# Order and halves of token block 2's output sums, and the engine of its y's lower parts, in a retention and feed-forward kernel

## The chip, the cores and the metric

The kernel runs on one core of a Trainium2 chip. The metric is device time in microseconds of one execution, as the median of several runs. In what follows TensorE is PE in the rows (PEld is its weight load), VectorE is DVE, ScalarE is ACT, GpSimd is POOL and SyncE is SP.

## What is computed

A linear attention with decay (2 batches, 8 heads, 768 positions, 64 features a head) gives x, and two feed-forward nets follow. Cut to what matters:

```python
def _moe_ref(x, w_in, w_out):            # x: 1536 x 512, w_in: 512 x 2048
    h = x @ w_in
    g = np.where(h >= 1, h, np.where(h <= -1, 0.0, (h + 1) ** 2 / 4))
    return g @ w_out                     # y: 1536 x 512

def _moe2_ref(y, w_a, w_b, w_out):       # w_a, w_b: 512 x 1536
    return ((y @ w_a) * (y @ w_b)) @ w_out

def reference(**inputs):
    x = attention(q, k, v, lam).transpose(0, 2, 1, 3).reshape(1536, 512)
    return _moe2_ref(_moe_ref(x))        # everything in float32
```

## The kernel before

**Precision.** A float32 number is carried as two tiles for TensorE: a high part (ScalarE casts it, line 265) and a low part, the remainder (line 266, a subtraction with two SBUF inputs, on GpSimd unless another engine is given). `split_act` issues the two one after the other. `mm3` (line 354) forms a product from three matmuls per pair: high by high, high by low, low by high. Every matmul of the feed-forward stages is issued at line 358; it has 128 rows, a 128x128 weight load of its own and 512 moving columns.

**Tokens.** The 1536 tokens are three blocks of 512 (nb = 0, 1, 2). Features are four groups of 128 (m or k = 0 to 3).

**PSUM.** There are eight banks of 512 columns. One (`words`) is a scratch for the weights' preparation. Seven are handed out in rotation by `bank()`; a product may start in its bank when the reader of the bank's content before has finished.

**First net.** `h_bank` makes one tile of g, `y_bank` (line 467) sums four tiles' contribution to one group m of y: 12 matmuls into a bank, then `gather` (line 464, VectorE) adds the bank to y's running sum in SBUF. In the last group of tiles (`last`) `y_bank` also splits the finished y of blocks 0 and 2 and half of block 1 into the tiles `block0` to `block2`, from which the second net's products read. Blocks 0 and 1 also go through `strassen_tokens` (lines 401 to 405), which prepares sums for a Strassen scheme.

**Second net.** From here on three of the seven banks are `held`: they collect the output of token block 2, m = 1, 2, 3, over all six groups, without a sum on VectorE. Four banks rotate. `both_banks` (line 413) makes one tile of g for all three blocks, in nine products: called s, u, a (block 2 with w_a, 12 matmuls), s again, w, f, b (block 2 with w_b, 12 matmuls), d, g in the order of issue; the others have six. VectorE adds at line 426, multiplies at 440, 444 and 451, and the result is split by `give_g`. `o_stage` (line 509) then calls `o_bank` (line 489) for m = 0, 1, 2, 3: six matmuls each. For blocks 0 and 1, and for block 2's m = 0, they go into a rotating bank and are gathered (line 464; in the first group line 462, a copy on ScalarE); for block 2's m = 1, 2, 3 they go into the held bank. The stage of block 2 for one group stands between the next group's two calls of `both_banks`; the last one ends the program. In the last group the sums are sent to the output: gathered ones as 128x512 on SyncE's queue (line 499), held ones as two halves, the first copied by VectorE and sent on SyncE's queue, the second copied by ScalarE and sent on ScalarE's (lines 506 and 507).

**Background.** The weights arrive as 64-bit numbers and are prepared tile by tile in small steps that `bg()` puts between the products: ScalarE at lines 280 and 281, VectorE at 294, 298, 302 and 311 (a custom instruction with two SBUF inputs), then a split; for pairs of tiles VectorE also forms four sums of 128x256 (line 333). Each engine takes its instructions in the order in which the code issues them, so the calls of `bg` set where these steps stand among the sums.

Of the kernel before, what the change touches and what calls it, by code (L numbers as in the profile page):

```python
# [22 lines left out]
DM = H * D  # L23
KT = DM // 128
NB = 3
# [10 lines left out]
def retention_ffn_kernel(ctx: ExitStack, tc: tile.TileContext, lam, att, w1i, w1o, w2ab, w2o, out):  # L36
# [7 lines left out]
    nc = tc.nc  # L44
# [16 lines left out]
    def bank():  # L61
        banks.rotate(-1)
        return banks[-1]
# [3 lines left out]
    def t2(name):  # L67
        return two.popleft()

    def free2(*tiles):  # L70
        two.extend(tiles)
# [60 lines left out]
    xy = {}  # L132
# [131 lines left out]
    def split_act(src, hi, lo, engine=None):  # L264
        nc.scalar.copy(hi, src)  # L265
        (engine or nc.gpsimd).tensor_tensor(out=lo, in0=src, in1=hi.bitcast(F32), op=ALU.subtract)  # L266
# [76 lines left out]
    def bg(n=1):  # L343

        for _ in range(n):
            if at["tile"] < min(at["limit"], len(order)):
                at["tile"] += next(stream)
# [6 lines left out]
    def mm3(ps, pairs, start=True, stop=True):  # L354
        n = len(pairs)
        for i, (l, r) in enumerate(pairs):
            for j, (a, b) in enumerate(((0, 0), (0, 1), (1, 0))):
                nc.tensor.matmul(out=ps, lhsT=l[a], rhs=r[b],   # L358
                                 start=(start and i == 0 and j == 0), stop=(stop and i == n - 1 and j == 2))
# [96 lines left out]
    acc = {}  # L456

    def gather(total, ps, first):

        if first:  # L460
            total = t2("acc")
            nc.scalar.copy(total, ps)
        else:
            nc.vector.tensor_tensor(out=total, in0=total, in1=ps, op=ALU.add)  # L464
        return total

    def y_bank(g, nb, m, last):
        ps = bank()
        fts = range(4 * g, 4 * g + 4)
        mm3(ps, [([wt["1o", f][:, a, m * 128:(m + 1) * 128] for a in range(2)],  # L470
                  [gt[1, f, nb][:, b, :] for b in range(2)]) for f in fts])
        y = acc["y", nb, m] = gather(acc.get(("y", nb, m)), ps, g == 0)
        if last:
            xy[nb] = [block[nb][:, k] for k in range(KT)]
            if nb != 1 or m >= 2:
                split_act(y, xy[nb][m][:, 0], xy[nb][m][:, 1])
            if nb == 2:
                free2(acc.pop(("y", nb, m)))

# [9 lines left out]
    def o_bank(g, nb, m, last):  # L489
        fts = range(2 * g, 2 * g + 2)  # L490
        r0 = nb * TB + m * 128
        pairs = [([gt[2, f, nb][:, a, m * 128:(m + 1) * 128] for a in range(2)],
                  [wt["2o", f][:, b] for b in range(2)]) for f in fts]
        if m not in held or nb < NB - 1:
            ps = bank()
            mm3(ps, pairs)
            o = acc["o", nb, m] = gather(acc.get(("o", nb, m)), ps, g == 0)
            if last:
                nc.sync.dma_start(out=out[r0:r0 + 128], in_=o)
            return  # L500
        mm3(held[m], pairs, g == 0, last)
        if last:
            o = t2("o")
            for i, copy, queue in ((0, nc.vector.tensor_copy, nc.sync), (1, nc.scalar.copy, nc.scalar)):
                cols = slice(i * DM // 2, (i + 1) * DM // 2)
                copy(o[:, cols], held[m][:, cols])
                queue.dma_start(out=out[r0:r0 + 128, cols], in_=o[:, cols])

    def o_stage(g, nb, pieces):
        last = g == FF2 // 256 - 1  # L510
        for m in range(KT):
            o_bank(g, nb, m, last)
            bg(pieces)
        for f in range(2 * g, 2 * g + 2):
            four.append(gt.pop((2, f, nb)))
            if nb == NB - 1:
                four.append(wt.pop(("2o", f)))
# [105 lines left out]
    def y_stage(g, nb, ms=range(KT), between=lambda m: None):  # L623
        for m in ms:
            y_bank(g, nb, m, g == FF1 // 512 - 1)
            between(m)
            bg()
        y_done(g, nb)

    y_stage(0, 0)  # L630
    for i in range(2, len(stages)):
        g, nb = stages[i]
# [16 lines left out]
    for g in range(groups):  # L649
        at["limit"] = 32 + 6 * g + 6  # L650
        done(32 + 6 * g + 2)
        both_banks(2 * g)
        at["limit"] = 32 + 6 * g + 8
        if g:
            o_stage(g - 1, 2, 2)
        done(32 + 6 * g + 4)
        both_banks(2 * g + 1)
        at["limit"] = 32 + 6 * g + 10
        done(32 + 6 * g + 6)
        o_stage(g, 0, 1)  # L660
        o_stage(g, 1, 1)
# [47 lines left out]
```

## Time and profile before

| what | us |
|---|---|
| runs: median (lowest to highest of 3) | 619.71 (618.56 to 620.05) |
| the profiled execution | 620.09 |
| its span in the trace | 618.3 |
| TensorE busy in it | 597.7 |
| VectorE busy in it | 457.3 |
| GpSimd busy in it | 278.5 |
| ScalarE busy in it | 267.8 |

The profiled execution's own time is 1.8 us longer than the span that the trace covers. Times in rows are counted from the span's start. A row of the timeline gives start, length, engine, line, operation, what it writes and reads, the shape, how many were merged, and in brackets how long the engine was idle before and what ended that. Matmuls are pipelined: a merged row's length is its last end less its first start, and starts show the pace.

### The profile page before, as it was taken

How to read it: one execution, taken by the hardware profiler on the slowest of the kernel's cores; microseconds unless marked ns; L12 is line 12 of the kernel's file. 1: busy time of each engine (PE TensorE's matmuls, PEld its weight loads, DVE VectorE, ACT ScalarE, POOL GpSimd, SP SyncE). 2: the span in 40 equal slices, each digit the busy share in tenths (PEclk: the TensorE clock that was granted, in tenths of full speed). 3: DMA queues.
4: the chain of work that ended last, by engine and by line, in shares of the span. 5: the costliest groups of instructions: out<-in, count | busy, mean ns of one | idle time of the engine just before them, and what ended most of it. 6: DMA issues, size and time to landing. Idle time of an engine off the chain costs nothing.

```text
span 618.3 us, 8380 instructions
## 1 busy us (share of the span) xinstructions
PE 597.7 (97%) x3100; PEld 488.4 (79%) x3100; DVE 457.3 (74%) x684; ACT 267.8 (43%) x473; POOL 278.5 (45%) x218
## 2 busy tenths in 40 slices
PE   7797899999999999999999999999999999999997
PEld 3676678888888888888888788888888888888886
DVE  1578861964975786497869997989979979979553
ACT  1245552655642553264545456434424424424110
POOL 3535570443522543352947655553453553543420
PEclk9799899999999999999999999999999999999999
DMA  5965520221310212131101222302302202300004
GB/s 176 378 247 203 184 92 1 75 96 68 103 64 10 98 68 69 34 103 49 55 1 35 68 87 83 103 34 90 95 21 96 92 18 93 100 14 1 0 23 182
DMA packets 20937, 52.72 MB, mean 85 GB/s; under 512 B 2584, under 2 KB 4896, under 8 KB 20896
## 3 DMA queue, kind: packets, MB, share of 16 engines
q1 hardware_dynamic: 19624, 51.52, 24.3%
q10 hardware_dynamic: 1272, 0.67, 0.4%
q8 instruction: 24, 0.39, 0.3%
q14 instruction: 17, 0.14, 0.1%
HBM read 49.03 MB, written 3.15 MB: 84 GB/s over the span
## 4 chain that ended last, share of the span: by engine, by line
PE 82%; DVE 8%; ACT 4%; POOL 2%; issue 2%; DMA 1%; ACTq 0%; DVEq 0%; POOLq 0%
PE ps L358 79%; DVE words L294 1%; PE ps L225 1%; PE ps L221 1%; DVE two L302 1%; DVE words L298 1%; DVE two L401 1%; DMA lamp<-in_lam 1%; ACT words L280 1%; DVE two L311 1%; PE ps L150 1%; DVE two L180 1%; DMA rows<-base 1%; ACT four L265 1%; ACT two L281 0%
## 5 line engine op out<-in xcount | busy, mean ns | idle before, releaser
L266 POOL TENSOR_TENSOR four<-two,four 128x512 fp32r<-128x512 f32 x109 | 143.1, 1319 | 213.6 <-ACT four L265 203.4
L358 PE MATMUL ps<-block,four 128*128 128x512 f32 x828 | 196.9, 391 | 1.4 <-POOL block L266 1.4
L358 PEld LDWEIGHTS ps<-block,four 128*128 128x128 f32 x828 | 154.6, 188 | 35.4 <-POOL block L266 1.8
L358 PE MATMUL ps<-four,four 128*128 128x512 f32 x633 | 162.0, 389 | 0.0
L358 PEld LDWEIGHTS ps<-four,four 128*128 128x128 f32 x633 | 118.7, 188 | 24.9 <-issue 0.2
L265 ACT CAST four<-two 128x512 fp32r<-128x512 f32 x109 | 67.1, 620 | 93.4 <-DVE two L451 23.7
L266 POOL TENSOR_TENSOR late_four<-two,late_four 128x512 fp32r<-128x512 f32 x47 | 62.2, 1329 | 56.8 <-ACT late_four L265 49.5
L358 PE MATMUL ps<-block,late_four 128*128 128x512 f32 x324 | 77.2, 389 | 0.0
L358 PEld LDWEIGHTS ps<-block,late_four 128*128 128x128 f32 x324 | 60.8, 188 | 12.6
L280 ACT ACTIVATE words<-raw 128x512 f32<-128x512 f32 x68 | 43.1, 634 | 55.0 <-DVE two L302 49.7
L358 PE MATMUL ps<-four,late_four 128*128 128x512 f32 x243 | 64.0, 389 | 0.0
L377 ACT ACTIVATE two<-two,half 128x512 f32<-128x512 f32 x42 | 30.2, 720 | 70.4 <-DVE two L376 70.4
L294 DVE TENSOR_SCALAR words<-words 128x512 f32<-128x512 f32 x68 | 47.0, 691 | 17.4 <-ACT words L280 17.4
L358 PE MATMUL ps<-late_four,four 128*128 128x512 f32 x213 | 58.5, 389 | 0.0
L358 PEld LDWEIGHTS ps<-four,late_four 128*128 128x128 f32 x243 | 45.6, 188 | 9.5
L464 DVE TENSOR_TENSOR two<-two,ps 128x512 f32<-128x512 f32 x62 | 42.2, 680 | 13.1 <-PE ps L358 13.1
L311 DVE CUSTOM_DVE_ANT_0 two<-two,two 128x1024 uint16<-128x1024 uint16 x54 | 49.7, 921 | 1.9
L376 DVE TENSOR_SCALAR two<-ps 128x512 f32<-128x512 f32 x42 | 28.7, 684 | 29.9 <-PE ps L358 29.4
L298 DVE TENSOR_SCALAR words<-words 128x512 int32<-128x512 int32 x68 | 47.5, 699 | 2.3
L426 DVE TENSOR_TENSOR two<-two,ps 128x512 f32<-128x512 f32 x50 | 32.9, 682 | 19.2 <-PE ps L358 16.7
L358 PEld LDWEIGHTS ps<-late_four,four 128*128 128x128 f32 x213 | 40.0, 188 | 8.3
L265 ACT CAST late_four<-two 128x512 fp32r<-128x512 f32 x47 | 28.9, 620 | 36.4 <-DVE two L440 11.4
(99 smaller groups left out, 596.3 us busy)
## 6 DMA issues: line engine op xcount, KB each, us to landing
load<-in_att SPq DMA_DIRECT2D x48, 256.0 KB, 5.3
raw<-in_w2ab SPq DMA_DIRECT2D x24, 512.0 KB, 3.2
raw<-in_w1i SPq DMA_DIRECT2D x16, 512.0 KB, 3.4
raw<-in_w1o SPq DMA_DIRECT2D x16, 512.0 KB, 3.3
raw<-in_w2o SPq DMA_DIRECT2D x12, 512.0 KB, 3.2
out<-two SPq DMA_DIRECT2D x7, 256.0 KB, 2.0
dmask<-rows SPq DMA_DIRECT2D x2, 256.0 KB, 4.6
out<-late_two SPq DMA_DIRECT2D x2, 256.0 KB, 2.0
```

Source lines behind the costliest of these rows:

```text
L150: nc.tensor.matmul(out=sc[c][h % 2][:, pr * CH:(pr + 1) * CH], lhsT=kT[p0:p0 + 64, pr * CH:(pr + 1) * CH], rhs=qT[p0:p0 + 64, pr * CH:(pr ...
L265: nc.scalar.copy(hi, src)
L266: (engine or nc.gpsimd).tensor_tensor(out=lo, in0=src, in1=hi.bitcast(F32), op=ALU.subtract)
L280: nc.scalar.activation(out=words, in_=r[:, :, 1].bitcast(F32), func=ACTF.Abs)
L294: nc.vector.tensor_scalar(out=words, in0=words, scalar1=HIGH_MIN, scalar2=HIGH_MAX, op0=ALU.max, op1=ALU.min)
L298: nc.vector.tensor_scalar(out=word, in0=word, scalar1=3, scalar2=0x3FFFFFFF, op0=ALU.logical_shift_left, op1=ALU.bitwise_and)
L311: nc.vector.tensor_tensor(out=v, in0=v, in1=c, op=ALU.add)
L358: nc.tensor.matmul(out=ps, lhsT=l[a], rhs=r[b], start=(start and i == 0 and j == 0), stop=(stop and i == n - 1 and j == 2))
L376: nc.vector.tensor_scalar(out=r, in0=ps, scalar1=-1.0, scalar2=1.0, op0=ALU.max, op1=ALU.min)
L377: nc.scalar.activation(out=r, in_=r, func=ACTF.Square, scale=0.5, bias=half)
L426: add = lambda o, x, ps: nc.vector.tensor_tensor(out=o, in0=x, in1=ps, op=ALU.add)
L464: nc.vector.tensor_tensor(out=total, in0=total, in1=ps, op=ALU.add)
```

## The change

Three things. In the last group `y_bank` gives block 2's low parts to VectorE and no longer to GpSimd. `o_stage` calls `o_bank` for m = 1, 2, 3, 0 and no longer 0, 1, 2, 3, for all blocks and groups; for blocks 0 and 1 all four go into rotating banks as before. And in the last group the sum of block 2's m = 0, now the program's last, is made in two halves of 256 columns, each in a bank of its own, with its own six matmuls, its own gather on VectorE and its own transfer, the first on SyncE's queue and the second on ScalarE's.

```diff
@@ -473,7 +473,7 @@
         if last:
             xy[nb] = [block[nb][:, k] for k in range(KT)]
             if nb != 1 or m >= 2:
-                split_act(y, xy[nb][m][:, 0], xy[nb][m][:, 1])
+                split_act(y, xy[nb][m][:, 0], xy[nb][m][:, 1], nc.vector if nb == 2 else nc.gpsimd)
             if nb == 2:
                 free2(acc.pop(("y", nb, m)))
 
@@ -492,11 +492,18 @@
         pairs = [([gt[2, f, nb][:, a, m * 128:(m + 1) * 128] for a in range(2)],
                   [wt["2o", f][:, b] for b in range(2)]) for f in fts]
         if m not in held or nb < NB - 1:
-            ps = bank()
-            mm3(ps, pairs)
-            o = acc["o", nb, m] = gather(acc.get(("o", nb, m)), ps, g == 0)
-            if last:
-                nc.sync.dma_start(out=out[r0:r0 + 128], in_=o)
+            parts = 2 if last and nb == NB - 1 else 1
+            for i in range(parts):
+                ps = bank()
+                cols = slice(i * DM // parts, (i + 1) * DM // parts)
+                mm3(ps[:, cols], [(l, [x[:, cols] for x in r]) for l, r in pairs])
+                if parts == 1:
+                    o = acc["o", nb, m] = gather(acc.get(("o", nb, m)), ps, g == 0)
+                else:
+                    o = acc["o", nb, m]
+                    gather(o[:, cols], ps[:, cols], False)
+                if last:
+                    (nc.scalar if i else nc.sync).dma_start(out=out[r0:r0 + 128, cols], in_=o[:, cols])
             return
         mm3(held[m], pairs, g == 0, last)
         if last:
@@ -508,7 +515,7 @@
 
     def o_stage(g, nb, pieces):
         last = g == FF2 // 256 - 1
-        for m in range(KT):
+        for m in (1, 2, 3, 0):
             o_bank(g, nb, m, last)
             bg(pieces)
         for f in range(2 * g, 2 * g + 2):
```

On VectorE, in the stage of y's last sums for block 2 (`block_73` is `block2`, `two_...` are y's running sums and weight tiles, `ps_112` to `ps_115` the four rotating banks):

```order
 L464 TENSOR_TENSOR two_93<-two_93,ps_112 128x512
+L266 TENSOR_TENSOR block_73<-two_93,block_73 128x512
 L294 TENSOR_SCALAR words<-words 128x512
 L298 TENSOR_SCALAR words<-words 128x512
 L464 TENSOR_TENSOR two_105<-two_105,ps_113 128x512
+L266 TENSOR_TENSOR block_73<-two_105,block_73 128x512
 L302 SCALAR_TENSOR_TENSOR two_109<-raw,words 128x512
 L464 TENSOR_TENSOR two_110<-two_110,ps_114 128x512
+L266 TENSOR_TENSOR block_73<-two_110,block_73 128x512
 L311 ISA two_109<-two_109,two_94 128x1024
 L464 TENSOR_TENSOR late_two_942<-late_two_942,ps_115 128x512
+L266 TENSOR_TENSOR block_73<-late_two_942,block_73 128x512
```

Each low part stands directly behind the sum of the same m, ahead of the next step on the weights and of the next sum.

On GpSimd, at the same place (`late_four_936` is the low part's tile of the weights that line 311 makes):

```order
 L405 TENSOR_TENSOR block_72<-two_108,block_72 128x512
-L266 TENSOR_TENSOR block_73<-two_93,block_73 128x512
-L266 TENSOR_TENSOR block_73<-two_105,block_73 128x512
-L266 TENSOR_TENSOR block_73<-two_110,block_73 128x512
 L266 TENSOR_TENSOR late_four_936<-two_109,late_four_936 128x512
-L266 TENSOR_TENSOR block_73<-late_two_942,block_73 128x512
 L266 TENSOR_TENSOR four_74<-two_99,four_74 128x512
```

The four low parts are gone, and the weight tile's low part follows the work on the Strassen sums.

On TensorE, at the program's end (`ps_116`, `ps_117` and `ps_111` are the held banks, `ps_113` and `ps_114` rotating ones):

```order
-L358 MATMUL ps_113<-late_four_937,four_76 128x512 x3
-L358 MATMUL ps_113<-four_86,four_77 128x512 x3
 L358 MATMUL ps_116<-late_four_937,four_76 128x512 x3
 L358 MATMUL ps_116<-four_86,four_77 128x512 x3
@@ -780,3 +778,7 @@
 L358 MATMUL ps_111<-late_four_937,four_76 128x512 x3
 L358 MATMUL ps_111<-four_86,four_77 128x512 x3
-L705 UNCONDITIONAL_BRANCH
+L358 MATMUL ps_113<-late_four_937,four_76 128x256 x3
+L358 MATMUL ps_113<-four_86,four_77 128x256 x3
+L358 MATMUL ps_114<-late_four_937,four_76 128x256 x3
+L358 MATMUL ps_114<-four_86,four_77 128x256 x3
```

The six matmuls of m = 0 leave the first place, and twelve of half the width end the program.

## Rows read from the trace of the kernel before

**Rows 1.** The page, part 1: busy us (share of the span) xinstructions.

```profile
PE 597.7 (97%) x3100; PEld 488.4 (79%) x3100; DVE 457.3 (74%) x684; ACT 267.8 (43%) x473; POOL 278.5 (45%) x218
```

**Rows 2.** Chain that ended last, in order of time: start, us, what; a long piece.

```profile
407.57 207.10 PE ps L358 x912
```

**Rows 3.** TensorE's waits (us, times, longest), then its timeline at the first both_banks.

```profile
PE ps L358 <- POOL block L266: 1.4, 1, 1.4
...
336.30 1.52 PE L358 MATMUL ps<-four,four 128*128 128x512 f32 x6
337.65 2.43 PE L358 MATMUL ps<-block,four 128*128 128x512 f32 x10
341.44 1.89 PE L358 MATMUL ps<-block,four 128*128 128x512 f32 x7 [1.36 <-POOL block L266]
```

**Rows 4.** Timeline of VectorE from the sum of m = 0 on.

```profile
332.55 0.68 DVE L464 TENSOR_TENSOR two<-two,ps 128x512 f32<-128x512 f32 x1
333.15 0.69 DVE L294 TENSOR_SCALAR words<-words 128x512 f32<-128x512 f32 x1
333.87 0.70 DVE L298 TENSOR_SCALAR words<-words 128x512 int32<-128x512 int32 x1
334.48 0.68 DVE L464 TENSOR_TENSOR two<-two,ps 128x512 f32<-128x512 f32 x1
335.08 0.68 DVE L302 SCALAR_TENSOR_TENSOR two<-raw,words 128x512 int32<-128x512 int32 x1
...
336.27 1.47 DVE L311 CUSTOM_DVE_ANT_0 two<-two,two 128x1024 uint16<-128x1024 uint16 x1
337.66 0.67 DVE L464 TENSOR_TENSOR late_two<-late_two,ps 128x512 f32<-128x512 f32 x1
338.26 0.69 DVE L294 TENSOR_SCALAR words<-words 128x512 f32<-128x512 f32 x1
...
340.92 1.02 DVE L311 CUSTOM_DVE_ANT_0 two<-two,two 128x1024 uint16<-128x1024 uint16 x1
```

**Rows 5.** Timeline of ScalarE: casts of m = 0 and 2, and what precedes.

```profile
333.26 0.62 ACT L265 CAST block<-two 128x512 fp32r<-128x512 f32 x1 [2.22 <-DVE two L464]
...
335.79 0.65 ACT L280 ACTIVATE words<-raw 128x512 f32<-128x512 f32 x1
...
336.91 0.62 ACT L265 CAST block<-two 128x512 fp32r<-128x512 f32 x1
```

**Rows 6.** Timelines of VectorE and GpSimd in strassen_tokens, the same subtraction.

```profile
323.06 0.68 DVE L405 TENSOR_TENSOR four<-two,four 128x512 fp32r<-128x512 f32 x1
323.83 1.61 DVE L405 TENSOR_TENSOR late_four<-two,late_four 128x512 fp32r<-128x512 f32 x1
...
323.27 1.62 POOL L405 TENSOR_TENSOR four<-two,four 128x512 fp32r<-128x512 f32 x1 [1.29 <-ACT four L403]
```

**Rows 7.** Timelines of VectorE and TensorE up to the second both_banks.

```profile
345.73 1.27 DVE L426 TENSOR_TENSOR two<-two,ps 128x512 f32<-128x512 f32 x2
...
351.00 0.68 DVE L444 TENSOR_TENSOR late_two<-late_two,ps 128x512 f32<-128x512 f32 x1
...
352.92 1.52 PE L358 MATMUL ps<-four,four 128*128 128x512 f32 x6
```

**Rows 8.** Timeline of the program's end, and a 128x256 sum from PSUM.

```profile
614.70 0.42 DVE L506 COPY two<-ps 128x256 f32<-128x256 f32 x1 [0.87 <-PE ps L358]
615.16 0.37 ACT L506 COPY two<-ps 128x256 f32<-128x256 f32 x1 [0.92 <-DVE two L506]
615.56 0.34 ACTq L507 DMA_DIRECT2D out<-two  x1
...
91.64 0.42 DVE L209 TENSOR_TENSOR st<-st,ps 128x256 f32<-128x256 f32 x1 [0.27 <-ACT st L208]
```

**Rows 9.** Weight loads by form (busy us, mean ns), and a timeline's row.

```profile
L358 PEld LDWEIGHTS ps<-four,late_four 128*128 128x128 f32 x243 | 45.6, 188 | 9.5
...
89.74 0.60 PEld L194 LDWEIGHTS ps<-load,two 128*64 128x64 f32 x16
```

## The prediction

> **What bounds the kernel now.** I read the busy time by engine first: TensorE is busy for 597.7 of the 618.3 us, VectorE for 457.3 [rows 1]. Then the chain that ended last: its last long piece is 207 us of matmuls without a break [rows 2]. Then TensorE's waits: of all matmuls of the feed-forward stages (line 358) one waited, for 1.36 us, and for GpSimd [rows 3]. So a change can win only that one wait, something at the very end, or less work on TensorE, and anything that makes TensorE wait is paid in full, because nothing behind it has slack to give back. The timelines around the wait and at the end show the rest.
>
> The wait: the last four banks of y (token block 2, features m = 0 to 3) are summed by VectorE (line 464), rounded to a high part by ScalarE (line 265, the cast), and the remainder is the low part (line 266, GpSimd). The third product of the first both_banks reads all four. It issues ten of its twelve matmuls at 337.65 and stands until GpSimd has the low part of m = 3; the eleventh starts at 341.44 [rows 3]. Ten matmuls at the pace of the row above it (six in 1.35 us, 0.226 each) would have ended at 339.92: TensorE loses 1.52 us here. VectorE is no less full: from 332.55 on its rows follow one another without a wait [rows 4].
>
> **Part 1: the low parts move to VectorE.** Off GpSimd go four instructions of about 1.3 us; onto VectorE come four of 0.68 us, the length of the same subtraction on VectorE where it was not disturbed [rows 6]. VectorE takes its queue in order, and each low part stands directly behind its own sum and needs the cast, which needs that sum. So VectorE stands still for each cast. Behind it in the queue are the next weight tile's steps and the next sum, and for the sums TensorE waits, since the products reuse those banks.
>
> The path, from the sum of m = 0 at 332.55 to 333.23 [rows 4], with 0.03 to 0.04 us for each hand-over (the sum ends at 333.23, the cast starts at 333.26) [rows 4, 5]:
> - cast 333.26 to 333.88 (0.62, unchanged) [rows 5]; low part of m = 0: 333.91 to 334.59.
> - Starts follow one another on VectorE by 0.60 after a sum, 0.72 and 0.61 across the two word steps (lines 294, 298) [rows 4]: word steps at 334.51 and 335.23, sum of m = 1 at 335.84 to 336.52. Cast to 337.17, low part 337.20 to 337.88.
> - Line 302 at 337.80, sum of m = 2 at 338.40 to 339.08 (0.60 each). ScalarE now does the next tile's lines 280 and 281, which waited for line 302; from the start of 280 to the cast of m = 2 is 336.91 - 335.79 = 1.12 us [rows 5], so from 338.51 the cast starts at 339.63 and ends at 340.25. Low part of m = 2: 340.28 to 340.96.
> - Line 311 at 340.88, this time undisturbed, sum of m = 3 at 341.48 to 342.16. ScalarE first casts the weight tile (341.6 to 342.2), then m = 3: to 342.82.
> - GpSimd starts the low part of that weight tile at about 342.25. Where two such instructions (both inputs in SBUF) meet on VectorE and GpSimd, one stands until the other is done: the subtraction that took 0.68 us took 1.61 beside a GpSimd instruction that had started before it [rows 6]. GpSimd is first here, by over half a microsecond. So the low part of m = 3 runs from about 343.51 to 344.19.
>
> TensorE's eleventh matmul then starts at 344.23 and not at 341.44: **+2.8 us**, in place of a wait that is shortened. That TensorE stands earlier as well (for the banks of m = 1 and m = 2, sums at 336.52 and 339.08, where the products would have come at 336.30 and 337.9) is inside this number. Bounds: without GpSimd in the way the low part starts at 342.85 and the term is +2.1; with a second instruction in the way it is 1.3 more, +4.1. I take 2.8, by the order and the row.
>
> **Part 2: what VectorE's delay does next.** After the low part come the same instructions as before, from line 294 (338.26) to line 311 (340.92), 2.66 us [rows 4]. They now start at 344.11; line 311 starts at 346.77, and ends at 347.46 where it ended at 341.94 (then 1.02 long). VectorE is 5.52 us late, TensorE 2.8. Until line 444 (351.00 to 351.68) no row of VectorE waited for TensorE. The first product that waits for line 444 is the second one of the next both_banks, which takes the bank that line 444 reads; it started at 352.92 [rows 7], with 1.24 us to spare. Now line 444 ends at 351.68 + 5.52 = 357.20, the product starts at 357.24: TensorE is **4.3 us** late in all, 1.5 more than at the first wait. This holds if the stretch between lines 311 and 444 keeps its length, with its two collisions with GpSimd: four short instructions of line 333 lie between 341.94 and the sum at 345.73 [rows 7], 3.8 us. They are put in motion by line 311 on both engines, so I expect them again. If both collisions go, that stretch is about 2.5 us shorter, VectorE's lateness is under 2.8 + 1.24, and the term is zero: bounds 0 and +1.5, taken +1.5. Later VectorE waits for TensorE again; from there on both are late by the same amount, and TensorE, without gaps, gives nothing back.
>
> **Part 3: the order of the sums.** In five of the six o_stages of block 2 the bank of m = 0 goes from first to last; 6 matmuls of 0.226 us change places with 18. On VectorE its sum moves behind six background steps, and on ScalarE, in the first of these stages, its copy. I cost this at nothing: the bank is wanted again by the fourth product of the next both_banks, 6 + 6 + 12 = 24 matmuls or 5.4 us after the last matmul of m = 0, and the six steps that VectorE now does first are ready while TensorE is still at the other three banks. If that cover were gone, each of the five stages would pay one sum of 0.68 us, 3.4 in all.
>
> **Part 4: the end.** Before, the last bank is one that is held: after the last matmul VectorE copies the first half (614.70, 0.42), ScalarE the second only after that (615.16, 0.37), and ScalarE's queue sends it at 615.56 [rows 8]. Now the last piece is half of the bank of m = 0, and its sum is one VectorE instruction of 128x256 with one input in PSUM: 0.42, as in line 209 [rows 8]. It is sent at 614.70 + 0.42 + 0.04 = 615.16: **-0.40 us**. Landing stays: the same two queues, 128 KB each. All copies of held banks, ScalarE's and SyncE's transfers move 1.36 us ahead of the end, and hide under the last matmuls.
>
> The price is TensorE's: twelve matmuls of 256 columns with twelve weight loads, in place of six of 512 with six. At half of 0.226 each they take the same 1.36 us. A weight load's row is 188 ns long, longer than 113; if loads could not overlap one another, twelve would take 2.26 us, +0.9. Against that stands the row of 16 loads of 64 columns in 0.60 us, 38 ns apart [rows 9], 75 for 128 columns. Bounds 0 and +0.9; I take **+0.1**, near that row. The Trainium skill ("TensorE: Matmul & The Clock Gate", the section on LDWEIGHTS and the mechanism in Part 3) has a load at columns / 1.2 ns, 107 for 128 columns, and lets it overlap a matmul only in another row group. By that, an estimate, the six added loads would cost 0.64 us, and the sum would be 0.5 higher. This trace does not agree for 512 columns, where six matmuls with their loads take 1.35 us.
>
> **Sum.** 2.8 + 1.5 + 0 - 0.4 + 0.1 = +4.0 us. The profiled execution took 620.09 us: 624.1. The median of the runs is 619.71, 0.38 lower: **623.7**. About 0.3%, 1.86 us, is what a measurement of this kernel can tell from no change: 617.85 to 621.57.
>
> **Rivals.**
> - A: the lateness of VectorE is caught up before line 444 (its collisions with GpSimd fall elsewhere). Then 2.8 - 0.3 = +2.5: 622.2. For it: GpSimd has four instructions fewer. Against it: the instructions that collide there are the same and start from the same event.
> - B, not slower: VectorE never stands, because ScalarE's casts are ready when it gets to them, and with GpSimd empty line 311 needs 0.69 and not 1.47 [rows 4]. Then the sum of m = 3 starts at 337.66 - 0.78 + 3 x 0.60 = 338.68, its low part ends at about 340.1, and of the 1.52 us only 0.2 is left. With the end: -1.3 - 0.3, 618.1; with the wait wholly gone 617.8. It decides at the instruction between sum and low part: with any two in between there would be time for the cast. The order has none, so I give it little.
> - C: as A, but the weight tile's low part does not get in front of that of m = 3. Then 2.1 - 0.3 = +1.8: 621.5, at the edge of what can be told from no change.
>
> **How the numbers follow.** Forecast 0.58, A 0.20, C 0.14, B 0.08. The likeliest's own range is 622.5 to 625.0 (its terms less 1.2, and 0.9 for the loads with some of the second collision). For 8 in 10 it must reach A and the upper part of C: 620.9 to 625.3. Slower by over 0.3%: forecast and A, 0.78. Within: C and part of B, 0.16. Faster: 0.06.
>
> **What would show it.** In the changed kernel's trace: VectorE idle before each of the four low parts until ScalarE's cast, about 0.7 us for m = 0 and 1, 1.3 and more for m = 2 and 3; TensorE's waits up to the eleventh matmul 4.3 us in all (1.52 before), and 1.5 more by the next both_banks; the last low part of y at 1.3 us or starting late behind GpSimd; the last transfer on ScalarE's queue 0.4 us sooner after the last matmul; twelve matmuls about 0.113 apart. I am wrong if VectorE starts a low part without a gap, or if TensorE's wait at that product is under 1.5 us.

## The result and the profile after

The changed kernel takes 625.70 us (median of 6, 624.83 to 626.60) against 619.88 us of the kernel before (6 runs beside it, 617.88 to 621.14). The ratio is 1.0099, with a 95% interval of 1.0082 to 1.0117: 6.1 us more, 5.1 to 7.3. The direction was forecast, the size was not: the sum said +4.0 us and the upper end of the range was 625.3.

One thing must be known to read the two traces side by side. The attention's first 95 us, which no edit touches, differ by up to 2.4 us between the profiled executions; in that of after, the feed-forward part starts 2.14 us sooner than in that of before, and the matmuls up to y's last sums all keep this difference. So the time of a row of after is compared here with its row of before less 2.14, which is called the row's old place. The profiled execution of after took 624.85 us, with a span of 623.1.

The page's first part, which answers to [rows 1]:

```profile
PE 599.0 (96%) x3106; PEld 487.7 (78%) x3106; DVE 462.5 (74%) x689; ACT 267.6 (43%) x473; POOL 273.6 (44%) x214
```

TensorE's waits in the feed-forward part (us in total, times, longest), which answer to the first line of [rows 3]:

```profile
PE ps L358 <- ACT two L428: 1.2, 2, 0.6
...
PE ps L358 <- ACT block L265: 1.1, 1, 1.1
PE ps L358 <- ACT words L280: 0.9, 1, 0.9
PE ps L358 <- DVE block L266: 0.9, 1, 0.9
PE ps L358 <- ACT late_two L428: 0.6, 1, 0.6
PE ps L358 <- DVE two L464: 0.2, 1, 0.2
```

One wait of 1.4 us for GpSimd has become seven. Four of them (L464, L280, the cast L265, L266) belong to y's last sums. The one put down to L280 ends at 337.12, 0.15 us behind VectorE's sum of m = 2 (not shown), whose bank the product takes; the first ends 0.14 behind the sum of m = 1. The other three name line 428, ScalarE's copy of product s, and come later, at 454.40, 501.53 and 548.66. The prediction has no word of line 428.

VectorE's timeline of after at y's last sums, from the sum of m = 0 on, which answers to [rows 4]; the last row is line 444 of [rows 7]:

```profile
330.42 0.68 DVE L464 TENSOR_TENSOR two<-two,ps 128x512 f32<-128x512 f32 x1
331.78 0.69 DVE L266 TENSOR_TENSOR block<-two,block 128x512 fp32r<-128x512 f32 x1 [0.69 <-ACT block L265]
...
338.16 0.69 DVE L266 TENSOR_TENSOR block<-two,block 128x512 fp32r<-128x512 f32 x1 [1.19 <-ACT block L265]
...
340.73 1.32 DVE L266 TENSOR_TENSOR block<-late_two,block 128x512 fp32r<-128x512 f32 x1 [0.69 <-ACT block L265]
...
354.38 0.68 DVE L444 TENSOR_TENSOR late_two<-late_two,ps 128x512 f32<-128x512 f32 x1
```

GpSimd's timeline there:

```profile
340.24 1.27 POOL L266 TENSOR_TENSOR late_four<-two,late_four 128x512 fp32r<-128x512 f32 x1 [8.59 <-issue]
```

TensorE's timeline there, which answers to [rows 3]; the last row is the product u of [rows 7]:

```profile
342.11 3.08 PE L358 MATMUL ps<-block,four 128*128 128x512 f32 x8 [0.86 <-DVE block L266]
344.99 2.19 PE L358 MATMUL ps<-four,four 128*128 128x512 f32 x6
...
355.21 1.62 PE L358 MATMUL ps<-four,four 128*128 128x512 f32 x6
```

VectorE idles before each low part until ScalarE has cast the sum just made (before that of m = 1, not shown, for 0.69 us). The last low part takes 1.32 and not 0.68, because GpSimd's instruction started 0.49 us before it and ended at 341.51. TensorE's eleventh matmul starts at 342.11; its old place is 341.44 - 2.14 = 339.30, so it is 2.81 us late. Its next matmuls are slow as well: six from 344.99 on span 2.19 us, where [rows 3] has 1.52 for six. The table of stretches shows why (from:to, the length, the busy time of PE, PEld, DVE, ACT and POOL, the granted clock, DMA share, GB/s):

```profile
341.00:342.90 1.90, 1.04 (x4) 0.67 (x4) 1.86 (x3) 0.19 (x1) 0.51 (x1) 1.00 0.00 0
342.90:346.40 3.50, 3.50 (x10) 2.74 (x9) 3.33 (x7) 2.25 (x5) 0.35 (x1) 0.51 0.35 121
346.40:348.00 1.60, 1.60 (x9) 1.29 (x8) 1.60 (x2) 0.58 (x2) 1.60 (x2) 1.00 0.18 69
```

The granted clock is 0.51, its lower level of 1.2 GHz, in the 3.5 us just behind the four waits, and back at 1.00 behind that. After that TensorE is 4.4 to 4.5 us behind its old place, and stays so until the first wait for line 428. Taken over the matmuls between the steps (medians over at least 170 starts), its lateness goes 4.54, 5.41, 6.28, 7.15: three steps of 0.87, 2.6 us in all.

The end, from the timeline of all engines, which answers to [rows 8]:

```profile
618.16 0.52 PE L358 MATMUL ps<-late_four,four 128*128 128x256 f32 x3
...
619.23 0.52 PE L358 MATMUL ps<-four,four 128*128 128x256 f32 x3
...
619.79 0.42 DVE L464 TENSOR_TENSOR two<-two,ps 128x256 f32<-128x256 f32 x1 [0.30 <-PE ps L358]
620.24 0.34 ACTq L506 DMA_DIRECT2D out<-two  x1
```

Nine half matmuls take 619.23 - 618.16 = 1.07 us, 0.119 each; from VectorE's last instruction to the last transfer's issue are 0.45 us, where [rows 8] had 0.86.

### The profile page after: what moved, and what is told of

It reads as the page before. It is cut to its first block, busy times and chain, and to the rows that moved or that the text cites. A ratio compares the mean times of both kernels' runs of the same rounds, so it can differ in the third digit from the quotient of the medians.

```text
span 623.1 us, 8399 instructions
## 1 busy us (share of the span) xinstructions
PE 599.0 (96%) x3106; PEld 487.7 (78%) x3106; DVE 462.5 (74%) x689; ACT 267.6 (43%) x473; POOL 273.6 (44%) x214
## 5 line engine op out<-in xcount | busy, mean ns | idle before, releaser
L266 POOL TENSOR_TENSOR four<-two,four 128x512 fp32r<-128x512 f32 x109 | 143.2, 1320 | 213.8 <-ACT four L265 202.4
L358 PE MATMUL ps<-four,four 128*128 128x512 f32 (+1 forms) x636 | 163.3, 390 | 1.4 <-ACT two L428 1.2
L265 ACT CAST four<-two 128x512 fp32r<-128x512 f32 x109 | 67.0, 619 | 94.4 <-DVE two L451 23.5
L266 POOL TENSOR_TENSOR late_four<-two,late_four 128x512 fp32r<-128x512 f32 x47 | 62.2, 1327 | 68.1 <-ACT late_four L265 50.0
L280 ACT ACTIVATE words<-raw 128x512 f32<-128x512 f32 x68 | 43.1, 634 | 56.4 <-DVE two L302 49.8
L358 PE MATMUL ps<-late_four,four 128*128 128x512 f32 (+1 forms) x216 | 58.7, 386 | 0.0
L464 DVE TENSOR_TENSOR two<-two,ps 128x512 f32<-128x512 f32 (+1 forms) x63 | 42.3, 672 | 17.0 <-PE ps L358 17.0
L265 ACT CAST late_four<-two 128x512 fp32r<-128x512 f32 x47 | 29.0, 621 | 40.1 <-DVE two L440 11.3
L426 DVE TENSOR_TENSOR two<-two,ps 128x512 f32<-128x512 f32 x52 | 34.2, 682 | 15.8 <-PE ps L358 12.1
```

The lines of the kernel that those rows point to most:

```text
L280: nc.scalar.activation(out=words, in_=r[:, :, 1].bitcast(F32), func=ACTF.Abs)
L358: nc.tensor.matmul(out=ps, lhsT=l[a], rhs=r[b], start=(start and i == 0 and j == 0), stop=(stop and i == n - 1 and j == 2))
L426: add = lambda o, x, ps: nc.vector.tensor_tensor(out=o, in0=x, in1=ps, op=ALU.add)
```

## Where the three late waits come from

Line 428 is ScalarE's copy of the bank of s, and product w takes that bank next. In ScalarE's queue the copy stands behind the casts of the weight sums that VectorE makes at line 333. The place is the stage of block 2 for the second group and the second call of both_banks around it; the same happens one and two groups later.

The timeline of all engines in the kernel before, at this place:

```profile
446.46 0.69 DVE L311 CUSTOM_DVE_ANT_0 two<-two,two 128x1024 uint16<-128x1024 uint16 x1
...
447.16 4.24 PE L358 MATMUL ps<-block,late_four 128*128 128x512 f32 x18
447.25 0.42 DVE L333 TENSOR_TENSOR two<-two 128x256 f32<-128x256 f32 x1
...
447.71 2.19 DVE L333 TENSOR_TENSOR two<-two,two 128x256 f32<-128x256 f32 x3
...
448.23 1.39 POOL L266 TENSOR_TENSOR four<-two,four 128x512 fp32r<-128x512 f32 x1 [1.68 <-PE ps L358]
...
449.94 0.62 ACT L265 CAST late_four<-two 128x512 fp32r<-128x512 f32 x1 [1.15 <-DVE two L333]
450.47 0.58 ACT L428 COPY late_two<-ps 128x512 f32<-128x512 f32 x1
...
451.24 1.54 PE L358 MATMUL ps<-four,late_four 128*128 128x512 f32 x6
```

The same in after, with the sum of m = 0 (line 464) now in between:

```profile
448.26 0.69 DVE L311 CUSTOM_DVE_ANT_0 two<-two,two 128x1024 uint16<-128x1024 uint16 x1
...
448.87 0.68 DVE L464 TENSOR_TENSOR two<-two,ps 128x512 f32<-128x512 f32 x1
...
449.46 0.42 DVE L333 TENSOR_TENSOR two<-two 128x256 f32<-128x256 f32 x1
449.56 4.24 PE L358 MATMUL ps<-block,late_four 128*128 128x512 f32 x18
449.92 0.43 DVE L333 TENSOR_TENSOR two<-two,late_two 128x256 f32<-128x256 f32 x1
450.02 1.48 POOL L266 TENSOR_TENSOR four<-two,four 128x512 fp32r<-128x512 f32 x1 [1.66 <-PE ps L358]
450.26 2.95 DVE L333 TENSOR_TENSOR two<-late_two,two 128x256 f32<-128x256 f32 x2
...
451.45 1.47 POOL L266 TENSOR_TENSOR late_four<-two,late_four 128x512 fp32r<-128x512 f32 x1
453.24 0.62 ACT L265 CAST late_four<-two 128x512 fp32r<-128x512 f32 x1 [2.24 <-DVE two L333]
453.77 0.58 ACT L428 COPY late_two<-ps 128x512 f32<-128x512 f32 x1
...
454.40 1.65 PE L358 MATMUL ps<-four,late_four 128*128 128x512 f32 x6 [0.60 <-ACT late_two L428]
```

Counted from line 311's start, GpSimd's subtraction begins at the same time (1.77 and 1.76 us later), but the first sum of line 333 begins 1.20 later and no more 0.79. In the trace before, the last three sums start at 447.71, 448.06 and 448.39: the second is done and the third under way when GpSimd starts at 448.23, and only the fourth stands behind it. The three take 2.19. Now the third stands behind GpSimd's first subtraction and the fourth behind its second: two sums take 2.95. The four end 4.95 us after line 311's start; before, it was 3.44. VectorE has gained 0.60 on TensorE, since the sum of m = 0 no longer precedes (line 311 starts 1.30 ahead of the 18 matmuls, and 0.70 before the change), so against TensorE the cast is 0.91 late. Before, the copy ended at 451.05 and the product started at 451.24, 0.19 later. 0.91 - 0.19 and a hand-over of 0.05 make 0.77; the product's start is late by 454.40 - (449.56 + 18 x 0.2267) = 0.76, and its first matmul adds the rest of the 0.87.

After the first group's stage the sum of m = 0 is a copy on ScalarE (line 462), and at the fifth there are no sums of line 333 left to make (the last one of the trace starts at 570.5), so only three of the five stages pay.

## Experiments

The kernel before took 619.53 us beside the first four (617.94 to 621.20) and 619.47 us beside the others (617.85 to 622.56). Times are given as the ratio to it with a 95% interval; what a trace shows is counted from the start of the feed-forward part, as above. The edits shown are cut to the lines that matter.

**The low parts alone.**

```diff
-                split_act(y, xy[nb][m][:, 0], xy[nb][m][:, 1])
+                split_act(y, xy[nb][m][:, 0], xy[nb][m][:, 1], nc.vector if nb == 2 else nc.gpsimd)
```

> Only the four low parts of block 2's y on VectorE; order and end as before. Theory: VectorE stands for each cast, the product a resumes 2.8 us later than before, and 1.4 to 1.5 us more follow, as slow matmuls (a granted clock of 0.5 in a stretch behind the wait) or as a wait for VectorE: +4.3 us in all, seven tenths of the whole loss. Rival: the low parts cost only the 2.8 us and the rest of the loss comes from the order and the clock is chance: +2.8.

623.74 us, ratio 1.0065 (1.0043 to 1.0086): +4.0 us. The four waits of y's last sums are there, and none for line 428. Its granted clock falls too, to 0.51 for 3.4 us. From before y's last sums to behind the second both_banks TensorE loses 4.50 us, and from there on nothing more. Parts 1 and 2 of the prediction had 4.3. The times alone (2.7 to 5.3) do not exclude the rival's +2.8; the 4.50 of the trace does.

**The order alone,** for all stages but the last group's:

```diff
-        for m in range(KT):
+        for m in range(KT) if last else (1, 2, 3, 0):
```

> Only the order 1, 2, 3, 0 in the stages of all groups but the last; low parts on GpSimd and the end as before. Theory: in the both_banks after block 2's stages of the groups 1, 2 and 3 TensorE waits for the copy of s (line 428) by 0.6 us on the page and 0.8 in the pace, three times: +2.4 us. Rival, the prediction's third part: no cost, 0.

622.67 us, ratio 1.0052 (1.0033 to 1.0071): +3.2 us. TensorE's waits in this kernel:

```profile
PE ps L358 <- ACT two L428: 1.5, 2, 0.9
PE ps L358 <- POOL block L266: 1.4, 1, 1.4
...
PE ps L358 <- ACT late_two L428: 0.6, 1, 0.6
```

The wait for GpSimd is that of [rows 3], and the three for line 428 are those of after. At the place told above, the timeline has the collision again:

```profile
448.05 2.95 DVE L333 TENSOR_TENSOR two<-late_two,two 128x256 f32<-128x256 f32 x2
```

TensorE's steps are 0.87, 1.22 and 0.87, 2.95 in all. At the second place line 311 starts only 0.95 ahead of the 18 matmuls (493.53 and 494.48) and not 1.30, which is the 0.35 that this step is longer; why it starts later there is not shown. So the order, costed at nothing, costs about 3 us by itself (2.0 to 4.4 by time), with low parts and end as they were.

**The end alone:** the halves of after, and the order 1, 2, 3, 0 in the last stage only.

```diff
-        for m in range(KT):
+        for m in (1, 2, 3, 0) if last and nb == 2 else range(KT):
```

> Only block 2's stage of the last group in the order 1, 2, 3, 0 with m = 0 in two halves; low parts on GpSimd, all other stages in the order 0, 1, 2, 3. Theory: the last transfer is issued 0.40 us sooner after the last matmul and the halves cost 0.1: -0.3 us, the only gain of the change. Rival: weight loads bound the halves, twelve matmuls 0.19 apart: +0.5.

618.41 us, ratio 0.9984 (0.9970 to 0.9998): -1.0 us, between -1.9 and -0.1. The predicted -0.3 lies inside, and the trace has -0.29; the rest of the 1.0 is not shown to come from the end. Low parts, order and end alone add up to 4.0 + 3.2 - 1.0 = 6.2 us, beside 6.1 for the whole change. With intervals this wide, so close a match is in part luck; in the traces it is 4.50 + 2.95 - 0.29 = 7.2 beside 6.9. (The order in the last group's stages of blocks 0 and 1, which the change alters too, is in none of the three.)

**Another order,** 1, 0, 2, 3: m = 0 still moves, but its sum does not come between line 311 and line 333.

```diff
-        for m in range(KT):
+        for m in range(KT) if last else (1, 0, 2, 3):
```

> As the run with the order alone, but the order is 1, 0, 2, 3: the sum of m = 0 then stands on VectorE between lines 302 and 311 of the first weight tile, and no longer between line 311 of the last tile and the four sums of line 333. Theory (a second collision of line 333 with GpSimd makes the cast behind it, and so the copy of s, late): one collision as before, no wait of TensorE for line 428, 0. Rival (a bank of m = 0 that is used later makes all of the next both_banks late): some of the loss stays, 0.3 or more at each of the three places, +1.

618.53 us, ratio 0.9994 (0.9980 to 1.0009): no difference that can be told. TensorE's waits in this kernel:

```profile
PE ps L358 <- POOL block L266: 1.4, 1, 1.4
...
PE ps L358 <- ACT two L433: 0.5, 1, 0.5
```

VectorE's timeline at the place told above:

```profile
445.85 2.19 DVE L333 TENSOR_TENSOR two<-two,two 128x256 f32<-128x256 f32 x3
```

There is one collision, of the same length as before the change, and no wait for line 428. In the trace TensorE loses 0.39 us once, at 405.94 in the first group, where the wait for line 433 (the copy of a) is, and at the three places at most 0.08. So not every change of order costs 3 us; this one leaves line 333 alone. But it also uses the bank of m = 0 earlier than the order 1, 2, 3, 0 does, so by itself it does not tell the place on VectorE from the bank.

**The sum behind all of line 333.** The next run keeps the bank last and moves the sum. If the collision is the cause, then the order 1, 2, 3, 0 with all eight weight steps ahead of the last bank should cost nothing.

```diff
-        for m in range(KT):
+        for m in range(KT) if last else (1, 2, 3, 0):
             o_bank(g, nb, m, last)
-            bg(pieces)
+            bg((pieces if nb < 2 or last else {1: 2, 2: 2, 3: 4, 0: 0}[m]))
```

> As the run with the order alone (1, 2, 3, 0), but all eight background steps stand ahead of the last bank, so that on VectorE the sum of m = 0 comes behind the four sums of line 333 and no longer between line 311 and them. TensorE's order is the same. Theory (the place of the sum among VectorE's instructions makes the second collision): no wait of TensorE for line 428, 0 us. Rival (the bank of m = 0 used last makes the next both_banks late): +3 as with the order alone.

620.10 us, ratio 1.0023 (1.0006 to 1.0040): +1.4 us, between the two. The timeline of all engines in this kernel, at the place told above:

```profile
445.71 4.46 PE L358 MATMUL ps<-block,late_four 128*128 128x512 f32 x18
446.00 1.85 DVE L333 TENSOR_TENSOR two<-late_two,two 128x256 f32<-128x256 f32 x2
...
447.78 0.67 DVE L464 TENSOR_TENSOR two<-two,ps 128x512 f32<-128x512 f32 x1
...
448.51 1.23 PEld L358 LDWEIGHTS ps<-block,late_four 128*128 128x128 f32 x6 [0.34 <-DVE two L464]
```

There is one collision again (1.85 for the third and fourth sum), and TensorE does not wait for line 428. But the sum of m = 0 now ends at 448.45, and the product that takes its bank waits for it: the 18 matmuls are 0.22 us longer than 4.24. TensorE loses 0.50, 0.19, 0.54 and 0.20 at four places, 1.4 in all. So my expectation failed by half: the collision explains the waits for line 428, and the cover by which I had costed the order at nothing, the bank, is itself too short once the sum stands behind the sums of line 333.

**The low parts one step later:** on VectorE, but each issued behind the sum of the next m, and the last behind two weight steps.

```diff
-            if nb != 1 or m >= 2:
+            if nb == 2:
+                nc.scalar.copy(xy[nb][m][:, 0], y)
+                if m:
+                    low_part(m - 1)
+            elif nb != 1 or m >= 2:
                 split_act(y, xy[nb][m][:, 0], xy[nb][m][:, 1])
...
+    def low_part(m):
...
+        nc.vector.tensor_tensor(out=lo, in0=acc["y", 2, m], in1=hi.bitcast(F32), op=ALU.subtract)
...
     y_stage(3, 2)
+    low_part(3)
```

> The four low parts on VectorE as in the change, but each issued behind the sum of the next m (the last behind two weight steps), so that the cast it needs is done when VectorE comes to it. Order and end as before. Theory: what costs is that VectorE stands for each cast, not the four subtractions; by the rows of before the last low part is done at about 341.3, TensorE goes on at 341.3 in place of 341.44, and VectorE's remaining lateness of 1.2 us lies within the 1.24 to spare: 0 us against before. Rival: four more subtractions of 0.68 us on a VectorE that is full cost what they take: +1.5 to +2.7.

619.36 us, ratio 0.9997 (0.9980 to 1.0013): no difference, and 4.2 us less than with the low parts directly behind their sums (in the traces 0.14 us lost in place of 4.50). VectorE's last low part in this kernel:

```profile
338.59 0.68 DVE L484 TENSOR_TENSOR block<-late_two,block 128x512 fp32r<-128x512 f32 x1
```

TensorE's matmul that needs the last one:

```profile
339.32 2.12 PE L358 MATMUL ps<-block,four 128*128 128x512 f32 x8 [0.97 <-DVE block L484]
```

Neither this low part nor the three ahead of it waits; TensorE waits 0.97 and not 1.36. Two or three other instructions now stand on VectorE between each sum and its low part. The work on VectorE is the same as with the low parts alone, so parts 1 and 2 are a cost of position, not of VectorE's added work.

**Spare matmuls.** Does the lower clock cost something of its own? To the kernel with the low parts alone I added twelve matmuls whose result is not used, four each ahead of the first product of block 2, of its last k, and of the matmul that needs the last low part.

```diff
...
+            filler(4)
+            mm3(ps, pairs[:3], True, False)
+            filler(4)
+            (l, r) = pairs[3]
+            nc.tensor.matmul(out=ps, lhsT=l[0], rhs=r[0], start=False, stop=False)
+            filler(4)
...
```

> As the run with the low parts alone, with twelve spare matmuls of 512 columns (four before the product a, four before its last k, four before the matmul that needs the last low part) into a held bank that nothing uses yet, so that TensorE does not stand idle while it waits; they change no result. Theory: VectorE's lateness of 5.5 us is what is paid in the end; the granted clock stays at 1.0, and TensorE waits for line 444 or line 440 about 1.5 us: +4.0 in all, as without the spare matmuls. Rival: the slow stretch of TensorE is a cost of its own; without it +2.8.

623.23 us, ratio 1.0068 (1.0050 to 1.0087): +4.2 us, as without them. Its table of stretches has the granted clock at 1.00 (from 336 us on; one stretch):

```profile
346.00:358.00 12.00, 11.13 (x47) 8.29 (x46) 11.55 (x18) 5.88 (x11) 6.94 (x5) 1.00 0.26 88
```

TensorE waits for VectorE instead, the longest time at product u, by its timeline (line 461 of this kernel is line 444 of the others):

```profile
356.64 1.63 PE L358 MATMUL ps<-four,four 128*128 128x512 f32 x6 [0.46 <-DVE late_two L461]
```

Product u starts 4.46 us late here and 4.42 with the low parts alone, where the clock fell; at the eleventh matmul it is 2.84 and 2.82. The lower clock spends time that TensorE would have stood waiting for VectorE.

**The end, and the wait of before.** The end alone won, so I took the one wait of [rows 3] away on top of it: in y's last stage the weight step between m = 2 and 3 moves behind m = 3.

```diff
-            bg()
+            if (g, nb, m) != (3, 2, 2):
+                bg(2 if (g, nb, m) == (3, 2, 3) else 1)
```

> The end of the change (the last stage in the order 1, 2, 3, 0, m = 0 in halves) with all else as before, but for one thing: no background step between y's sums of m = 2 and m = 3 (two behind m = 3 instead), so that on GpSimd the low part of m = 3 stands ahead of the weight tile's. Theory: TensorE's one wait of 1.52 us goes down to 0.2, the end gives 0.3 to 0.4 more: -1.6 us. Rival: the weight tile's low part, 1.3 us later, becomes what TensorE waits for: -0.4, the end alone.

618.31 us, ratio 0.9982 (0.9967 to 0.9997): -1.1 us, where I expected -1.6. The timeline of all engines in this kernel, TensorE's two products and GpSimd's two low parts:

```profile
335.58 4.66 PE L358 MATMUL ps<-block,four 128*128 128x512 f32 x18
...
336.79 1.30 POOL L266 TENSOR_TENSOR block<-late_two,block 128x512 fp32r<-128x512 f32 x1
...
338.04 1.30 POOL L266 TENSOR_TENSOR late_four<-two,late_four 128x512 fp32r<-128x512 f32 x1
```

The low part of m = 3 now precedes that of the weights, and the eighteen matmuls of both products run in 4.66 us, 0.42 more than eighteen without a gap. In the trace TensorE gains 1.24 us at the eleventh matmul and gives 0.29 back at the second both_banks. The whole trace, counted from the start of the feed-forward part, is 1.24 us shorter than that of before, and 0.95 shorter than that of the end alone. The median is only 0.1 below that of the end alone, which these times can't tell from nothing; the shortest five of twelve took 616.64 to 616.90, the shortest six of twelve with the end alone 617.59 to 617.76. By the trace this is the fastest version of the study, which the medians do not show, and the low parts and the order of the change have no part in it.

## Why the prediction was right and wrong

**Part 1, +2.8: right.** Its starts for the low parts of m = 0, 1 and 2 less 2.14 are 331.77, 335.06 and 338.14; the rows have 331.78, 335.08 (not shown) and 338.16. The end of the last was put at 344.19, in its new place 342.05, and 340.73 + 1.32 is 342.05. The eleventh matmul is 2.81 late. GpSimd stood in the way as costed, so rival C falls; VectorE stood before all four, so rival B falls. Two of the signs were named too large: VectorE's idle time before m = 2 and 3 is 1.19 and 0.69 where 1.3 and more was named, and the four waits of TensorE add up to 3.14 where 4.3 was named; by the starts of the matmuls its loss is 1.52 + 2.81 = 4.3. The Trainium skill ("SBUF — State Buffer", the section on who interferes with whom) says that issue order decides which of VectorE and GpSimd blocks; the 1.32 in place of 0.68, behind a GpSimd instruction that began 0.49 sooner, agrees.

**Part 2, +1.5 more: right in size, and reached in another way than told.** Line 444 starts at 354.38; its old place is 351.00 - 2.14 = 348.86, so VectorE is 5.52 late, the number of the prediction, and rival A falls. TensorE starts product u at 355.21, 4.43 late; forecast was 4.3. But it lost the 1.6 us between by running at the lower clock, and not by a wait for line 444. The spare matmuls show that the limit was line 444 all the same.

**Part 3, 0: this is the step that failed.** I wrote: "I cost this at nothing: the bank is wanted again by the fourth product of the next both_banks, 6 + 6 + 12 = 24 matmuls or 5.4 us after the last matmul of m = 0, and the six steps that VectorE now does first are ready while TensorE is still at the other three banks." The bank held in after, as told: TensorE has no wait for it there. What was not looked at is the two steps behind the sum: the sum pushes the sums of line 333 into GpSimd's second subtraction, and they are followed by a cast that stands ahead of the copy of s, which had 0.19 us to spare. So three stages that were put at nothing pay 0.87 each, 2.6 us (with the order alone 2.95 in the trace and 3.2 by time). The bound of that part, 3.4, would have held it, but its mechanism was another one, the chance given to it was none, and it was not carried into the range.

**Part 4, -0.4 and +0.1: right.** The twelve half matmuls are 0.119 apart and take 0.07 us more than six full ones. The Trainium skill's price for the loads ("TensorE: Matmul & The Clock Gate", the section on LDWEIGHTS), taken without overlap as the prediction took it, would by that estimate have put 0.64 there; the trace does not agree, since load and matmul together take 0.119. (The Trainium skill's section on the mechanism, on the same page, which the prediction names too, also has a load into a background weight buffer pulled ahead of running matmuls; the prediction left that out.) The last transfer comes 0.86 - 0.45 = 0.41 sooner after VectorE's last start.

**The sum.** In the traces, counted from the same start of the feed-forward part, it is 4.54 + 2.61 + 0.07 - 0.40 = 6.8 us, beside 6.1 (5.1 to 7.3) of the medians; the two whole traces differ by 6.9. Without part 3 it would be 4.2, beside the 4.0 that was forecast.

## What to carry to other kernels

When an instruction moves in an in-order queue, cost not only the wait for its own result: write down what stands behind its new place, what that meets on the engine it shares a path with, and who is next in the queue of the engine behind that; then look for the smallest slack among these, here 0.19 us. A step that needs another engine's answer to the instruction just ahead of it should not stand directly behind it; two or three other instructions between were worth 4 us here, with the same work on the same engine. A cover that is named must be the one that ends first, and a bound that has been worked out belongs in the range until a row excludes it.

## What the runs showed of the hardware

- A shift of 0.41 us between VectorE and GpSimd turned one collision, of a VectorE sum with a GpSimd subtraction that both read two SBUF inputs, into two: three sums of 128x256 took 2.19 us before and two took 2.95 after, where the first of the four, undisturbed, took 0.42. In [rows 6] such a meeting made a subtraction of 0.68 take 1.61.
- The granted clock fell to its lower level for a stretch of 3.5 us (0.51) behind four waits of 0.22, 0.95, 1.11 and 0.86 us; the single wait of 1.36 in [rows 3], and one of 0.97 with the low parts one step later, left it at 1.00. With spare matmuls in these waits it stayed at 1.00, and the kernel took the same time.
- A matmul of 256 columns with a 128x128 weight load of its own took 0.119 us in a row of twelve, half of the 0.226 of 512 columns, though the load's row is 188 ns long [rows 9].
